# Three leading blocks' V by SyncE's queue in fp32 with a cast, and a new order of the first 340 tasks

## The chip, the core and the metric

The kernel runs on one core of one Trainium2 chip. A core has TensorE (PE) for matmuls, VectorE (DVE), ScalarE (ACT) and GpSimd (POOL) for the rest, SyncE (SP), which here only issues DMAs, and 16 DMA engines that all DMA queues share. PE writes its results to eight banks of PSUM, 128 x 512 fp32 each; DVE or ACT must empty a bank before it is used again. Every engine works through its own instructions strictly in order and waits at the first one whose inputs are not ready.

The metric is the time of one execution on the device in microseconds (us), lower is better.

## The reference

Eight heads of sliding-window attention with ALiBi, whose output goes as tokens into a feed-forward layer with squared ReLU:

```python
batch, n_heads, seq, head_dim = (8, 8, 576, 64)       # q, k, v in fp32
scores = scale * np.matmul(q, k.transpose(0, 1, 3, 2))
rel = pos[:, None] - pos[None, :]
bias = slopes[:, None, None] * (-np.abs(rel).astype(np.float32))[None, :, :]
mask = (rel >= 0) & (rel < 128)
scores = np.where(mask, scores + bias[None], -1000000000.0)
attn = np.exp(scores - np.max(scores, axis=-1, keepdims=True))
attn = attn / (np.sum(attn, axis=-1, keepdims=True) + 1e-09)
x = np.matmul(attn, v).transpose(0, 2, 1, 3).reshape(4608, 512)
h = x @ w_in                                          # 512 x 2048
out = np.maximum(h, 0.0) ** 2 @ w_out                 # 2048 x 512
```

## The kernel before

**Tiling.** Each sequence of 576 positions is cut into blocks of up to 128 positions by all 8 heads; the blocks are numbered in the order in which they are worked on. Blocks 0 to 3 are the first blocks of four sequences. They have no earlier block to look at and are called lone. Later blocks are "full" (they also look at the block before) or "half". The 4608 tokens are taken in nine groups g of 512 for the feed-forward layer. Group 0 (and with it blocks 0 to 3) is computed directly, in unit pieces; group 1 by unit pieces of twice the width; from group 2 on the first matrix product, and for all groups the second, is done by Strassen's seven products, with weight sums (us, ws) and token sums (ut, S1 to S4) made by DVE.

**Names of tasks.** Every piece of work is a task with a name; m is a block, g a group.

- `lk`, `lq`, `lv` load K, Q, V of a block. POOL's loads cast from fp32 to bf16 on the way. Block 0's K and Q go by SP's and ACT's queues in fp32 into a stage buffer (a part of the tile wsum), two halves each (`lk0.0`, `lk0.1`, `lq0.0`, `lq0.1`), and are cast by `ck0` and `cq0`.
- `tp m.0` and `tp m.1` transpose K and Q of a block on PE (four 128x128 matmuls each), `ev m.0.0` and `ev m.1.0` copy them out of PSUM.
- `b m` writes a lone block's ALiBi bias into two banks (two 128x512 matmuls); `s m` adds the scores, and for full blocks `s m.0` and `s m.1` are two bursts. `e m.i` is the exponential on ACT (lone: two; full: four), `m m.i` the multiplication by a mask on DVE for full blocks. The masks themselves (`mask part.head`) are 16 exponentials on ACT.
- `pv m.0`, `pv m.1` multiply by V, each for half of the heads; `r` and `n` are reciprocal and normalisation on DVE; `xp` transposes the result on PE and `x` copies it into xT.
- `u g.r.e` is a unit piece of x @ w_in: in group 0 r is one of four 128-token ranges, and e one of the pieces of w_in (2, 2, 4, 4, 4 chunks of 128 columns for r = 0; four of 4 chunks for the others). `relu...` is its ReLU on ACT, `squ...` its square.
- `w_in0` to `w_in4` load these pieces of w_in by POOL (two of 256 KB, three of 512 KB in bf16), `w_out0` to `w_out3` load w_out.
- `p g.i.z` is a Strassen product of the second matrix product.

**What sets the order.** The whole order is written out by hand in one string, ORDER, with a letter for the engine and the number of a PSUM bank or buffer (`s4.0::7,2`, `reluu0.1.0:a:0`). The planner takes the tasks in that order, checks that nothing comes before what it needs, and emits them; each engine's instruction stream is the part of ORDER with its letter. So a task that stands early in ORDER and waits for a load holds up everything behind it on its engine.

**Places that the steps touch.** PE starts with 12 warm-up matmuls (`warm`, line 662). Bias, scores and exponentials of lone blocks are lines 805, 814 and 823, transposes of K and Q 690, pv 874, xp 921, unit pieces 1021, their ReLU 988; copies go through a helper (428 on DVE, 430 on ACT). Block 0's stage loads are line 585, other K and Q loads of the first blocks 610, V loads 621, w_in 543, w_out 546. V of the blocks 0 to 3 has tiles of its own (vf), with a column of ones per head set by `one0.m`. K and Q of a block lie in a ring of four buffers (kq), so that the fifth block's load waits for the first block's transposes.

Of the kernel before, what the change touches and what calls it, by code (L numbers as in the profile page):

```python
# [25 lines left out]
N_XP = 13  # L26
N_CUT = 0
# [36 lines left out]
slope1.1:d slope0.1:a slope1.3:a ck0:a slope0.2:a warm::0 b0::1,2 lk2:g lq2:g lq0.0:s lq0.1:s lk1:g cq0:a one0.0:d  # L64
tp0.0::0 tp2.0::3 b2::4,5 tp0.1::6 tp2.1::7 ev2.0.0:d ev0.1.0:a lk3:g lq1:g tp3.0::3 ev3.0.0:a ev2.1.0:d ev0.0.0:d
one0.2:d tp1.0::6 s2 s0 e0.0:a e2.0:a e2.1:a ev1.0.0:d e0.1:a lv0:g lv2:g lq3:g lv1:g w_in1:g w_in0:g w_in2:g lv3:g
w_in3:g lk4:g lq4:g b1::0,3 tp1.1::6 pv2.0::4 ev1.1.0:d r2.0:d pv0.0::6 pv0.1::2 s1 n2.0:d r0.1:d r0.0:d n0.0:d
tp3.1::4 n0.1:d xp0.0::2 pv2.1::6 x0.0:d r2.1:d ev3.1.0:d mask1.1:a e1.0:a e1.1:a table:a pv1.0::0 pv1.1::3 b3::5,1
n2.1:d u0.0.1::2 r1.0:d r1.1:d n1.0:d n1.1:d xp2.0::6 s3 u0.0.0::0 xp1.0::3 dist0:d x2.0:a e3.0:a x1.0:a mask1.7:a
reluu0.0.0:a:0 u0.2.0::6 mask0.3:a mask1.2:a mask0.1:a mask1.6:a e3.1:a u0.1.0::3 u0.1.1::0 pv3.0::1 pv3.1::5  # L70
u0.2.1::4 u0.0.2::7 squ0.0.0:d one1.2:d reluu0.1.0:a:0 mask0.2:a reluu0.2.0:a:1 one1.8:d r3.0:d squ0.1.0:d one1.7:d
r3.1:d n3.0:d n3.1:d xp3.0::5 x3.0:d one1.5:d reluu0.2.1:a:0 one1.6:d squ0.2.1:d squ0.2.0:d reluu0.1.1:a:2 mask1.5:a
# [40 lines left out]
reluf2.2.4:a:0 sqf2.2.4:d sqc22.2.3:d c12.2.3:d:0 sqc12.2.3:d S2.2.0:d sqf2.1.4:a pv17.1::5 pv17.0::4 reluf2.3.4:a:3
sqf2.3.4:a st1.2.1:s st0.2.0:s st1.3.1:s st0.2.1:s st1.2.0:s st1.3.0:s kqT18:s x14:s x13:s x15:s x16:s kqT20:s kqT21:s
kqT22:s s18.0::1,2 s18.1::0,7 p2.2.0::3 p2.2.1 S1.2.1:d S2.2.1:d r17.0:d S4.2.1:d S3.2.1:d r17.1:d n17.0:d e18.0:a
e18.1:a s1_2:a:3 S3.2.0:d n17.1:d m18.0:d p2.5.0::2 p2.6.0 p2.5.1 p2.6.1 f3.0.1::5 f3.0.2::4 f3.1.1::1 s2_2:d:7
e18.2:a e18.3:a s1.3.0:a:5 ut3.0:d ut3.1:d m18.1:d ut3.2:d c11.3.0:d:0 ut3.3:d c11_2:d f3.0.5::7 f3.0.6 s2.3.0:a:1
# [198 lines left out]
def kernel(  # L316
    ctx: ExitStack, tc: tile.TileContext, q, k, v, moe_w_in, moe_w_out, out
):
    nc = tc.nc

    B, H, S, D = q.shape
    d_model = moe_w_in.shape[0]
# [88 lines left out]
    def tile_of(slot):  # L411
        return tiles[slot.tag][slot.idx]
# [110 lines left out]
    t_one = {}  # L523
# [39 lines left out]
    def load_block(m, key, v_key=None):  # L563
# [56 lines left out]
        def fetch_v():  # L620
            nc.gpsimd.dma_start(tile_of(s_v[m])[0:n, :, 0:D], source(v, m))  # L621
# [859 lines left out]
```

## Time and profile before

| | us |
|---|---|
| median of 3 runs (lowest to highest) | 287.59 (287.37 to 289.48) |
| the profiled execution | 288.0 |
| its span, first to last instruction | 285.9 |

| engine | busy us | share of the span |
|---|---|---|
| POOL | 106.3 | 37% |
| POOL's DMA queue | 18.10 MB | 87.8% of 16 engines' span |
| SP's DMA queue | 20.00 MB | 41.1% of 16 engines' span |

The busy time of a group of instructions counts pipelined matmuls in full, so a busy PE is not a PE at its peak: the time of a stretch of PE work is better read from the starts of what follows. The shares of the DMA queues add up the times of packets of which one engine has several under way, and so go over 100% in stretches. In POOL's timeline the time of a load is that of issuing it; when it has landed is told by the issues' median time to landing. A row such as `10.97 2.06 ACT ... x4 [0.65 <-PE s L814]` has start, length, engine, line, what is written from what, the count, and in brackets the idle time of the engine before it and what ended it.

### The profile page before, as it was taken

To read this page: it belongs to the slowest core of one execution; us is meant where nothing else is said; L and a number is where in the kernel's file an instruction comes from. 1 tells how busy PE (TensorE), PEld (TensorE's weight loads), DVE (VectorE), ACT (ScalarE), POOL (GpSimd) and SP (SyncE) were. 2 spreads that over 40 slices of the span, in tenths; PEclk is the share of its full clock that TensorE was granted. 3 is DMA by queue.
4 is the path that set the end of the run, shared out by engine and by line. 5 is a ranking of instruction groups with operands and counts; after the bars stand their busy time and mean duration, and the time that the engine had idled before them with its cause. 6 is when DMAs were issued, how large, how long until landed. Compare 5 with 4: busy or idle time off the path is not lost.

```text
span 285.9 us, 8500 instructions
## 1 busy us (share of the span) xinstructions
PE 277.0 (97%) x3403; PEld 240.0 (84%) x3404; DVE 247.1 (86%) x566; ACT 207.5 (73%) x408; POOL 106.3 (37%) x132
## 2 busy tenths in 40 slices
PE   6799999999999999999999999999999999999994
PEld 2588999888888888898888888889889888888883
DVE  2555898799999999999999899998999979998752
ACT  4579978986588993879779958686898655657300
POOL 8977645576567026580266253430000000000000
PEclk9999999999999999999999999999999999999998
DMA  9999999999999999999999999997531220031124
GB/s 126 161 197 167 183 201 165 171 172 148 206 145 250 131 172 129 149 207 130 203 135 150 139 174 164 170 164 157 148 93 39 40 73 3 0 111 39 53 79 127
DMA packets 169062, 39.08 MB, mean 137 GB/s; under 512 B 154560, under 2 KB 169024, under 8 KB 169024
## 3 DMA queue, kind: packets, MB, share of 16 engines
q0 software_dynamic: 115184, 18.10, 87.8%
q1 hardware_dynamic: 53248, 20.00, 41.1%
q8 instruction: 26, 0.43, 0.7%
q10 hardware_dynamic: 592, 0.46, 0.6%
q14 instruction: 12, 0.10, 0.1%
HBM read 36.70 MB, written 9.44 MB: 161 GB/s over the span
## 4 chain that ended last, share of the span: by engine, by line
PE 95%; ACT 2%; DVE 1%; issue 0%; POOL 0%; DVEq 0%; POOLq 0%
PE o L1271 38%; PE h L1116 30%; PE h L1021 9%; PE s L745 6%; PE pv L874 5%; PE wm L662 2%; PE xp L921 1%; PE tp L690 1%; ACT P L823 1%; ACT rt L988 1%; PE pv L856 1%; PE o L1373 0%; PE s L805 0%; ACT masks L475 0%; PE pv L851 0%; PE s L814 0%
## 5 line engine op out<-in xcount | busy, mean ns | idle before, releaser
L1271 PEld LDWEIGHTS <-g 128*128 128x128 bf16 x704 | 67.3, 98 | 9.0
L777 ACT ACTIVATE P<-s 128x512 bf16<-128x512 f32 x120 | 64.7, 613 | 5.7 <-PE s L745 3.3
L430 ACT ACTIVATE f<-h 128x512 f32<-128x512 f32 x74 | 42.5, 601 | 25.8 <-PE h L1116 25.5
L1137 DVE CUSTOM_DVE_ANT_0 rt<-h,f 128x512 bf16<-128x512 f32 x84 | 56.4, 684 | 4.9 <-ACT f L430 1.7
L980 ACT ACTIVATE g<-rt 128x512 bf16<-128x512 bf16 x79 | 48.4, 634 | 6.4 <-DVE rt L1137 5.9
L1271 PE MATMUL o<-w_out_sb,g 128*128 128x256 bf16 x432 | 52.3, 273 | 0.0
L1116 PE MATMUL h<-xT,w_in_sb 128*128 128x256 bf16 x336 | 46.9, 273 | 0.0
L1116 PEld LDWEIGHTS <-w_in_sb 128*128 128x128 bf16 x448 | 42.2, 98 | 5.6
L616 POOL DMA_DIRECT2D kq<-in_k_dram x24 | 21.5, 895 | 57.7 <-DMA kqT<-kq 54.7
L988 ACT ACTIVATE rt<-h 128x512 bf16<-128x512 f32 (+1 forms) x61 | 35.2, 599 | 8.6 <-PE h L1116 3.9
L1271 PE MATMUL o<-wsum,sums 128*128 128x256 bf16 x288 | 35.5, 273 | 0.0
L1116 PEld LDWEIGHTS <-us 128*128 128x128 bf16 x336 | 31.9, 98 | 4.3 <-DVE ut L1085 0.2
L1271 PE MATMUL o<-wsum,g 128*128 128x256 bf16 x272 | 34.5, 273 | 0.0
L772 DVE TENSOR_TENSOR P<-P,masks 128x1024 bf16<-128x1024 bf16 x48 | 32.2, 680 | 1.3 <-ACT masks L475 0.8
L1116 PE MATMUL h<-ut,us 128*128 128x256 bf16 x224 | 31.1, 273 | 0.0
L1021 PE MATMUL h<-xT,w_in_sb 128*128 128x128 bf16 (+1 forms) x384 | 30.8, 237 | 0.1
L982 DVE TENSOR_TENSOR g<-rt 128x512 bf16<-128x512 bf16 (+1 forms) x66 | 26.1, 413 | 4.7 <-ACT rt L988 4.4
L1271 PEld LDWEIGHTS <-sums 128*128 128x128 bf16 x288 | 27.5, 98 | 3.1
L901 DVE TENSOR_TENSOR x<-pv,rec 128x256 bf16<-128x256 f32 x72 | 28.7, 417 | 0.7
L1021 PEld LDWEIGHTS <-w_in_sb 128*128 128x128 bf16 x384 | 27.0, 98 | 2.3 <-issue 0.2
L621 POOL DMA_DIRECT2D vt<-in_v_dram x28 | 25.0, 908 | 7.8 <-PE pv L856 5.3
L430 ACT ACTIVATE f<-o 128x512 f32<-128x512 f32 x29 | 17.3, 599 | 11.0 <-PE o L1271 10.0
(84 smaller groups left out, 378.1 us busy)
## 6 DMA issues: line engine op xcount, KB each, us to landing
out_dram<-f SPq DMA_DIRECT2D x62, 128.0 KB, 3.9
kq<-in_k_dram POOLq DMA_DIRECT2D x31, 128.0 KB, 6.4
kq<-in_q_dram POOLq DMA_DIRECT2D x31, 128.0 KB, 7.2
vt<-in_v_dram POOLq DMA_DIRECT2D x28, 128.0 KB, 7.5
w_out_sb<-in_moe_w_out_dram POOLq DMA_DIRECT2D x4, 512.0 KB, 11.6
w_in_sb<-in_moe_w_in_dram POOLq DMA_DIRECT2D x3, 512.0 KB, 8.6
out_dram<-f SPq DMA_DIRECT2D x15, 64.0 KB, 2.1
vf<-in_v_dram POOLq DMA_DIRECT2D x4, 128.0 KB, 4.9
```

The costliest lines, as they stand in the source:

```text
L430: nc.scalar.activation(o, i, AF.Copy)
L621: nc.gpsimd.dma_start(tile_of(s_v[m])[0:n, :, 0:D], source(v, m))
L772: nc.vector.tensor_tensor(flat(Pt[sP.idx], w), flat(Pt[sP.idx], w), flat(mk, w), op=ALU.mult)
L777: nc.scalar.activation(flat(Pt[sP.idx], slice(2 * i, 2 * i + 2)), sS[i].tile.rearrange("p (j t) -> p j t", j=2)[:, :, lo:hi], AF.Exp, bias ...
L901: nc.vector.tensor_tensor(o, heads(sv)[0:n, :, 0:D], sr.tile[0:n, :].unsqueeze(2).to_broadcast([n, 4, D]), op=ALU.mult)
L980: nc.scalar.activation(o, i, AF.Square, bias=0.0, scale=1.0)
L982: nc.vector.tensor_tensor(o, i, i, op=ALU.mult)
L988: nc.scalar.activation(rts[srt.idx][:, 0:n], slot.tile[:, 0:n], AF.Relu, bias=0.0, scale=1.0)
L1021: nc.tensor.matmul(slot.tile[:, f * w:(f + 1) * w], w_in_sb[:, cc, fc * 128:(fc + 1) * 128], xT[:, cc, lo % (XR * 128):lo % (XR * 128) + w ...
L1116: nc.tensor.matmul(slot.tile[:, j * 256:j * 256 + 256], a, b_, start=fresh and j == 0 and c == 0, stop=c == 1, skip_group_check=True)
L1137: nc.vector._custom_dve(TENSOR_ADD_SAT, out=rts[srt.idx], in0=slot.tile, in1=other(), s0=FMAX, s1=0.0)
L1271: nc.tensor.matmul(slot.tile[:, z * 256:z * 256 + 256], stationary(c), moving(c), start=fresh and z == 0 and c == 0, stop=c == F - 1, skip ...
```

## The change

Two things change.

First, V of the blocks 0, 2 and 1 is no longer loaded and cast by POOL's queue. It is loaded by SP's queue in fp32 into stage buffers 1 to 3 (other parts of wsum), by one DMA per block in pieces of 256 bytes, and then cast to bf16 by a new task, `cv m`, on ACT (blocks 2 and 0) or DVE (block 1).

```diff
+V_HW = (0, 2, 1)
...
         def fetch_v():
             nc.gpsimd.dma_start(tile_of(s_v[m])[0:n, :, 0:D], source(v, m))
+        if m in V_HW:
+            st, s_sv = stages[1 + V_HW.index(m)][:, 0:d_model], Slot(f"stage{1 + V_HW.index(m)}")
+            l_v = plan.add({"SP": 720.0}, key + 0.2 if v_key is None else v_key,
+                           lambda: nc.sync.dma_start(st[0:n].rearrange("s (h d) -> s h d", h=H), source(v, m)), [],
+                           [s_sv], dma=700.0, lat=1500.0, name=f"lv{m}")
+            c_v = plan.add({"DVE": 590.0, "ACT": 480.0}, key + 0.2 if v_key is None else v_key,
+                           lambda: copy(c_v, tile_of(s_v[m])[0:n, :, 0:D], st[0:n].rearrange("s (h d) -> s h d", h=H)),
+                           [l_v], [s_v[m]], [s_sv], name=f"cv{m}")
+            t_load[m] = c_v
+            t_v[m] = [c_v, t_one["v0", m]]
+            return
```

Second, ORDER is rewritten up to the first products of group 0's second matrix product, about 340 tasks. Behind that the tasks and their order are the same; PSUM banks and a few buffers are renumbered throughout, consistently. POOL's loads now stand in this order:

```diff
-lk2 lq2 lk1 lk3 lq1 lv0 lv2 lq3 lv1 w_in1 w_in0 w_in2 lv3 w_in3 lk4 lq4 lk5 lk6 lq5 lv5 lq6 w_in4 lk7 lv4 lv6 lq7
-w_out3 w_out0 lv7 w_out2 w_out1 lkq8 lkq12 lkq9 lkq10
+lk2 lq2 lk1 lq1 lk3 lq3 w_in0 lv3 lk5 lq5 w_in1 lk4 lq4 w_in2 w_in3 lk7 lk6 lq6 w_in4 lv4 lv5 lq7
+w_out3 lv7 w_out2 lv6 w_out1 lkq8 lkq9 w_out0 lkq12 lkq10
```

PE's first tasks:

```diff
-warm b0 tp0.0 tp2.0 b2 tp0.1 tp2.1 tp3.0 tp1.0 s2 s0 b1 tp1.1 pv2.0 pv0.0 pv0.1 s1 tp3.1 xp0.0 pv2.1 pv1.0 pv1.1 b3
-u0.0.1 xp2.0 s3 u0.0.0 xp1.0 u0.2.0 u0.1.0 u0.1.1 pv3.0 pv3.1 u0.2.1 u0.0.2 xp3.0 u0.1.2 tp4.0 tp4.1 u0.2.2 s4.0 s4.1
+warm b0 tp0.0 tp0.1 b2 tp2.0 tp2.1 tp1.0 s0 tp1.1 s2 tp3.0 tp3.1 pv0.0 pv0.1 b1 s1 b3 pv2.1 xp0.0 pv1.0 s3 pv2.0 pv1.1
+tp5.0 pv3.0 xp2.0 pv3.1 u0.0.0 u0.0.1 tp5.1 tp4.0 xp1.0 u0.2.0 tp4.1 xp3.0 u0.1.0 s5.0 s4.1 s4.0 u0.3.0 s5.1 u0.2.1
```

ACT's, from the second cast of block 0's Q on:

```diff
-cq0 ev0.1.0 ev3.0.0 e0.0 e2.0 e2.1 e0.1 mask1.1 e1.0 e1.1 table x2.0 e3.0 x1.0 mask1.7 reluu0.0.0 ...
+cq0 cv2 ev0.1.0 cv0 ev0.0.0 e0.0 e0.1 e2.0 e2.1 ev3.1.0 e1.0 e1.1 mask1.1 mask1.0 e3.0 x0.0 e3.1 mask1.3 x2.0 ev5.0.0 ...
```

DVE's, up to block 0's normalisation:

```diff
-one0.0 ev2.0.0 ev2.1.0 ev0.0.0 one0.2 ev1.0.0 ev1.1.0 r2.0 n2.0 r0.1 r0.0 n0.0 n0.1
+one0.0 ev2.0.0 ev2.1.0 ev1.0.0 one0.2 cv1 ev3.0.0 ev1.1.0 r0.0 r0.1 n0.0 n0.1
```

Farther back in the rewritten part, the products p0.2, p0.1 and p1.1 of the second matrix product stand between the last unit pieces of group 1 instead of behind them, and some evacuations and squares change between ACT and DVE.

More of the change, by code (lines that the diff above doesn't have):

```diff
@@ L63 @@
 iota:g ident:d dist1:d slope1.0:d warm0:d lk0.1:a lk0.0:s one0.1:d slope0.3:d slope1.2:a slope0.0:a one0.3:d
[L64 to L72, printed above, removed]
@@ L113 @@
[L113 to L117, printed above, removed]
@@ L193 @@
-c11.8.2:d:0 c22.8.2:d:1 sqc11.8.2:a f8.2.4 sqc22.8.2:a c12.8.2:d:0 S1.8.0:d S3.8.0:d sqf8.0.4:d sqc12.8.2:d S1.8.1:d
-S2.8.0:d S3.8.1:d s5_7:a:1 reluf8.2.4:a:1 s2_7:a:6 p8.1.0::7 p8.1.1 p7.7.0 p7.7.1 sqf8.2.4:a c22_7:d s1_8:a:4
-sqf8.3.4:a p8.2.0::1 p8.2.1 c11_8:d S2.8.1:d p7.4.0 p7.4.1 p8.6.0 p8.6.1 p8.5.0::1 p8.5.1 st6.4.3:s st6.3.1:s
+slope1.1:d slope0.1:a slope1.3:a ck0:a slope0.2:a warm::0 b0::1,2 lk2:g lq2:g lq0.0:s lq0.1:s lv0:s lv2:s tp0.0::0
+cq0:a tp0.1::3 cv2:a b2::4,5 ev0.1.0:a one0.0:d lk1:g lq1:g lk3:g lq3:g lv1:s tp2.0::6 ev2.0.0:d tp2.1::7 cv0:a
@@ new lines @@
+ev2.1.0:d ev0.0.0:a tp1.0::3 s0 e0.0:a e0.1:a ev1.0.0:d one0.2:d cv1:d w_in0:g lv3:g lk5:g lq5:g w_in1:g lk4:g lq4:g
+tp1.1::3 s2 e2.0:a e2.1:a tp3.0::0 tp3.1::1 pv0.0::7 ev3.0.0:d pv0.1::2 ev3.1.0:a ev1.1.0:d b1::6,0 s1 e1.0:a e1.1:a
+b3::4,3 r0.0:d r0.1:d n0.0:d n0.1:d mask1.1:a pv2.1::5 xp0.0::2 pv1.0::6 r2.1:d r1.0:d s3 mask1.0:a e3.0:a pv2.0::1
+pv1.1::0 r2.0:d x0.0:a n2.0:d n2.1:d tp5.0::7 n1.0:d e3.1:a pv3.0::4 xp2.0::5 pv3.1::3 u0.0.0::6 u0.0.1::2 r1.1:d
+n1.1:d r3.0:d n3.0:d r3.1:d dist0:d tp5.1::0 mask1.3:a x2.0:a ev5.0.0:a tp4.0::7 xp1.0::4 u0.2.0::5 tp4.1::1 n3.1:d
@@ new lines @@
+x1.0:d xp3.0::3 u0.1.0::4 ev4.1.0:d ev5.1.0:d w_in2:g w_in3:g lk7:g lk6:g lq6:g w_in4:g lv4:g lv5:g lq7:g w_out3:g
+lv7:g w_out2:g lv6:g w_out1:g lkq8:g lkq9:g mask0.6:a reluu0.0.0:a:0 mask1.7:a ev4.0.0:a mask0.5:a mask0.2:a
+reluu0.2.0:a:1 mask1.6:a reluu0.0.1:a:2 reluu0.1.0:a:3 mask0.0:a x3.0:d squ0.2.0:d s5.0::0,1 e5.0:a s4.1::3,5
+s4.0::2,7 u0.3.0::6 e4.0:a mask1.5:a mask0.7:a e4.2:a mask0.1:a squ0.0.0:d s5.1::0,4 u0.2.1::2 u0.0.2::3 e5.1:a
+reluu0.2.1:a:0 reluu0.3.0:a:1 mask1.4:a mask1.2:a e4.1:a mask0.4:a one1.7:d u0.3.1::2 squ0.2.1:d e5.2:a mask0.3:a
@@ new lines @@
+s2.2.2:a:7 s17.1::0,1 f2.3.6 f2.1.4 f2.2.7 s5.2.2:a:2 e17.2:a f2.2.3 f2.3.5::0 sqc12.2.1:d sqc11.2.2:d S1.2.0:d
+s2.2.3:a:3 c22.2.2:d:3 sqc11.2.3:d reluf2.1.4:a:0 s5.2.3:a:2 f2.3.7 c12.2.2:d:1 c22.2.3:d:2 e17.3:a sqc22.2.2:a
+sqc12.2.2:d m17.1:d m17.0:d p2.1.0::7 f2.2.4 f2.3.4 p2.1.1 f2.3.3 s3_1:a:2 reluf2.2.4:a:1 sqf2.2.4:d sqc22.2.3:d
+c12.2.3:d:1 sqc12.2.3:d S2.2.0:d sqf2.1.4:a pv17.1::4 pv17.0::5 reluf2.3.4:a:3 sqf2.3.4:a st1.2.1:s st0.2.0:s
+st1.3.1:s st0.2.1:s st1.2.0:s st1.3.0:s kqT18:s x14:s x13:s x15:s x16:s kqT20:s kqT21:s kqT22:s s18.0::2,1 s18.1::6,3
@@ new lines @@
+m37.0:d s1.6.3:a:2 e38.0:a e38.1:a e38.3:a c11.6.3:d:1 sqc11.6.3:d m37.1:d m38.0:d s1.6.2:d:2 p5.4.0 f6.3.6 f6.2.2::6
+f6.3.5::2 pv37.0::4 pv37.1::1 c11.6.2:d:1 s2.6.3:a:3 f6.3.7 r37.1:d f6.2.6 p5.4.1 f6.2.5::6 e38.2:a s5.6.3:a:1
+c22.6.3:d:0 m38.1:d r37.0:d n37.0:d n37.1:d s2.6.2:a:2 sqc11.6.2:a f6.2.7 f6.3.3 st4.4.3:s x31:s x32:s st5.2.1:s
+st5.2.0:s st4.3.0:s x33:s st4.3.1:s st4.4.2:s x34:s s5.6.2:a:1 c22.6.2:d:1 f6.2.3 sqc22.6.3:a sqf6.0.4:a c12.6.2:d:0
+c12.6.3:d:2 f7.0.1::1 pv38::4,3 s3_5:a:1 sqc12.6.2:a f6.3.4 f7.1.1::7 pv36.0::2 r38.0:d n38.0:d r38.1:d n38.1:d
```

228 lines of the change are left out of this document (112 added, 116 removed).

## The prediction, made before the change was run

> **What bounds the kernel now.** I read the page first (span, shares, chain), then the stages, then PE's timeline of the first 33 us, then ACT's, then the landings of the first loads.
>
> ```profile
> span 285.9 us, 8500 instructions
> PE 277.0 (97%) x3403; PEld 240.0 (84%) x3404; DVE 247.1 (86%) x566; ACT 207.5 (73%) x408; POOL 106.3 (37%) x132
> PE 95%; ACT 2%; DVE 1%; issue 0%; POOL 0%; DVEq 0%; POOLq 0%
> 10.00:15.00 5.00, 3.39 (x61) 2.37 (x61) 2.91 (x11) 3.75 (x9) 5.00 (x8) 1.00 1.90 171
> 30.00:35.00 5.00, 5.00 (x116) 4.60 (x109) 4.04 (x15) 5.00 (x12) 3.24 (x5) 1.00 1.97 176
> ```
>
> TensorE is the bound, with 95% of the chain. The two rows of stages (length, then busy PE, PEld, DVE, ACT, POOL, then clock, DMA share, GB/s) say where it isn't full: 3.39 of 5 us in 10 to 15, all of it by 30. The reordered tasks hold the same matmuls, and the order behind them stays. So the change can move the end only by how much PE time it loses, mostly before about 32 us. To count that loss I need prices, from PE's timeline and (last five rows) the chain of waits:
>
> ```profile
> 2.50 5.17 PE L662 MATMUL wm<-sums 128*128 128x512 bf16 x12 [2.50 <-DVE sums L448]
> 7.50 0.60 PE L805 MATMUL s<-sums,ident 128*128 128x512 bf16 x2
> 7.93 0.61 PE L690 MATMUL tp<-ident,kq 128*128 128x128 bf16 x8
> 10.20 0.74 PE L814 MATMUL s<-kqf 64*128 64x128 bf16 x16
> ```
>
> ```profile
> 17.67 2.68 PE h L1021 x48
> 28.50 0.89 PE h L1021 x16
> 29.84 0.69 PE s L745 x16
> 32.09 1.89 PE h L1021 x32
> 37.64 0.48 PE pv L874 x16
> ```
>
> A bias pair b takes 0.43 (7.50 to 7.93), a transposing group tp or xp of four 0.225 (8.38 minus 7.93 is 0.45 for eight), a lone block's scores 0.37, a pv half 0.12 when eight matmuls become four, a unit piece u of four chunks 0.89 and of two 0.45, a full block's score burst 0.345. Warm-up ends at 7.50 in either order. At 17.67 PE had done 4 b, 8 tp, 4 lone s, 6 pv, 3 xp and 2 short u: 1.72+1.80+1.48+0.72+0.68+0.90 = 7.30 us. It had taken 10.17, so 2.87 were lost. At 32.09, with 4 b, 14 tp, 4 s, 8 pv, 4 xp, 2 short and 11 long u and 6 bursts (20.97 us), 3.62 were lost. Hence the ceiling of any gain: 3.6 us, and less than that by what ACT allows.
>
> **The change, part by part.** Three fp32 loads of V (blocks 0, 2, 1) go to SyncE's queue behind the q halves, and leave POOL's. Three casts are added: cv2 and cv0 on ACT, cv1 on DVE. On ACT the order becomes cq0, cv2, ev0.1.0, cv0, ev0.0.0, e0.0: SyncE's second load now stands ahead of the first block's evacuations.
>
> ```profile
> 2.10 0.60 SPq L585 DMA_DIRECT2D wsum<-in_q_dram  x1
> wsum<-in_q_dram SPq DMA_DIRECT2D x1, 128.0 KB, 4.2
> 1.34 1.02 POOL L610 DMA_DIRECT2D kq<-in_k_dram  x1 [0.16 <-issue]
> kq<-in_k_dram POOLq DMA_DIRECT2D x1, 128.0 KB, 5.1
> q0 software_dynamic: 854, 0.11, 84.6%
> q1 hardware_dynamic: 236, 0.22, 38.9%
> q0 software_dynamic: 4876, 0.62, 241.4%
> 5.82 0.92 POOL L621 DMA_DIRECT2D vf<-in_v_dram  x1
> vf<-in_v_dram POOLq DMA_DIRECT2D x1, 128.0 KB, 4.9
> 9.28 1.57 POOL L543 DMA_DIRECT2D w_in_sb<-in_moe_w_in_dram  x2
> w_in_sb<-in_moe_w_in_dram POOLq DMA_DIRECT2D x1, 256.0 KB, 5.7
> w_in_sb<-in_moe_w_in_dram POOLq DMA_DIRECT2D x1, 256.0 KB, 6.3
> 63.83 0.68 DVE L1341 TENSOR_TENSOR f<-o,f 128x512 f32<-128x512 f32 x1
> ```
>
> *The loads.* The second q half, issued at 2.10, landed at 6.3; POOL's first load, issued at 1.34, at 6.44, and its sixth, issued at 5.82, at 10.7: 0.86 apart, at POOL's issue rate. The third queue row (8 to 12 us) gives the engines' own rate: 4876 packets in 4 us, 1024 (one block's 128-byte pieces) in 0.84. In 3.25 to 5.25 (the two queue rows before it) the queues used 123.5% against 241.4% when full: half the engines' time, 0.97 us, was free. Three V loads are 3 x 1024 pieces of 256 bytes. At the same 0.84 each they need 2.52, 0.97 of it free, so POOL's loads behind them come 1.55 later than POOL's own rate would give: q3, the sixth, at 12.3. Then w_in0 (256 KB: two such pieces, issued at 9.28 and 10.02, landed at 15.0 and 16.3, so 1.34 each), v3, k5, q5 (0.84 each) and w_in1: 12.3+1.34+2.52+1.34 = 17.5. Without the free time it is 18.5, with V costing nothing 16.0.
>
> The Trainium skill ("DMA: Bandwidth & Descriptors", Issuing engines are not separate DMA queues) says that DMAs of all issuing engines run on the same 16 engines and interleave, so that spreading them saves issue time only. By it the V loads cost their full 2.52, w_in1 lands at 18.5, 0.1 after PE's arrival below, and the sum would be 288.6. It speaks against the change; the row of stores beside POOL's loads, below, agrees with it.
>
> *When V lands.* No row shows a SyncE load of 1024 pieces. From below: issued behind q0.1 at about 2.7 (lv0) and 3.4 (lv2) with q's 4.2, lv2 lands at 7.6. From above, the two nearest kinds on that queue:
>
> ```profile
> q1 hardware_dynamic: 582, 0.54, 104.7%
> q0 software_dynamic: 17, 0.00, 2.0%
> out_dram<-f SPq DMA_DIRECT2D x1, 128.0 KB, 4.9
> out_dram<-f SPq DMA_DIRECT2D x3, 128.0 KB, 1.8
> L676 SPq DMA_TRANSPOSE kqT<-kq x7: 1232/1934/3269, 47.4 to 69.2; - x7
> DMA to landing us min/median/max: 5.2/6.8/8.5
> ```
>
> A store of 128 KB lands in 1.8 us when POOL's queue is empty (200 to 205 us) but in 4.9 beside it (83 us); in 88 to 89.5 us SyncE's packets ran nearly alone (582 to 17) while POOL's stood. So the engines serve roughly by order of issue, and a load waits for what was issued before it. A transpose of kq takes 1.2 us at least to issue and 5.2 to 8.5 to land: lv2 issued at 4.0 would land at 9.2 to 12.5. I take 9.3: q0.1's 6.33, three loads of 0.84 (lv0, lv2 and one of POOL's between), and half of another. The bounds for lv2 are 7.6 and 12.5.
>
> *ACT and PE from there.*
>
> ```profile
> 6.41 0.63 ACT L430 ACTIVATE kq<-wsum 128x512 bf16<-128x512 f32 x1 [1.50 <-DMA wsum<-in_q_dram]
> 9.23 1.09 ACT L430 ACTIVATE kqf<-tp 128x512 bf16<-128x512 bf16 x2 [2.20 <-PE tp L690]
> 10.97 2.06 ACT L823 ACTIVATE P<-s 128x512 bf16<-128x512 f32 x4 [0.65 <-PE s L814]
> 22.50 1.30 ACT L475 ACTIVATE masks<-sums 128x128 bf16<-128x128 f32 x6
> 39.63 1.13 ACT L777 ACTIVATE P<-s 128x512 bf16<-128x512 f32 x2
> 54.74 1.04 ACT L430 ACTIVATE kqf<-masks 128x1024 bf16<-128x1024 bf16 x1
> ```
>
> A 128x512 pass paces at 0.515 (2.06/4), a mask at 0.2. The first fp32 cast took 0.63, about as long. cv2 starts at 9.35; with ev0.1.0, cv0 and ev0.0.0 behind it (4 x 0.5) ACT is through at 11.35, where the old order ended its two evacuations at 10.3. s0 runs at 11.55, e0.0 starts at 12.1. Seven passes (four e, ev3.1.0, e1.0, e1.1) and two masks take it to 16.1. e3.0 needs s3, which PE's order puts behind pv1.0, and so behind e1.0 (15.2): s3 is out by then. With e3.0, x0.0 and e3.1 it is 17.7. Then pv3.1, u0.0.0 (0.45), and u0.0.1 starts at 18.4; w_in1 (17.5) is there. By then PE has done 4 b, 9 tp, 4 s, 8 pv, 2 xp and one short u: 7.09 us in 10.9, 3.81 lost against 2.87 at 17.67 before. That is +0.94.
>
> *What costs nothing.* cv1 (0.68, by DVE's fp32 sum above) waits for lv1 with ev3.0.0 and ev1.1.0 queued behind it on DVE; k3 lands only at about 11.4, so about 1 us of cover; beyond that every us goes to s1. POOL loses three issues of 0.9, but its landings follow the engines. SyncE has nothing behind lv1 until its first transpose at 47. The stage buffers lie in wsum, whose next writers, the weight sums, come after the units. Later loads, with a 512 KB piece as twice 1.34: w_in2 21.9, w_in3 24.5, w_in4 29.7, v4 30.6, each ahead of its user: before u0.3.3, the first to need w_in4, PE has 19.4 us of work, so it is there at 7.5+19.4+3.8 = 30.7, and at pv4.0 two long u later. Between 18 and 32 I let the loss grow as before (0.75).
>
> **The sum.** The profiled execution took 288.0 (span 285.9 and 2.1 around it), 0.4 above the median 287.59. 288.0 + 0.94 = 288.94, less 0.4: 288.5.
>
> **Rivals.**
> *B, V in time.* If lv2 is there at 8.5, ev0.1.0 starts when tp0.1 is out (8.38 and 0.2), ev0.0.0 is through 1.25 earlier, u0.0.1 starts at 17.15 if w_in1 is there, and 2.56 are lost: 0.3 better than before. With no growth between 18 and 32 it is 1.05 better. 286.5 to 287.3, say 286.9. For it: engines half free until 5.25. Against: three loads' 2.5 us, and w_in1 at 17.5. More isn't in it: from 8.58 ACT has 7 us of passes before pv3.1, so even this order can't save 2.9 us.
>
> *C, V late, ACT blocked.* The price is one for one: each us of lv2 after 9.3 moves ev0.1.0, s0, all exps and u0.0.1. Beyond 11.3 it costs over 1% (0.94+2.0). By the transposes' median lv2 lands at 10.8 (+2.4), by their worst at 12.5 (+4.1). PE would then stand nearly idle from 9.1 to over 12, and the warm-up shows what a cold array costs: 12 matmuls of 512 in 5.0 us, 0.42 each, against 0.215 for the same shape right after 7.50. One such slow stretch adds about 1 us. 290.5 to 292.5, say 291.5. For it: the trace's transposes, and packets of one queue standing while the other's run. Against: q0.1's 4.2 at the very moment.
>
> On that clock the Trainium skill ("TensorE: Matmul & The Clock Gate", Part 1) says that an idle window of about 3.4 us halves it; by that the slow stretch would be at least that long. The trace has no such window behind the warm-up to show it: PE's 3.39 of 5 us in 10 to 15 went at clock 1.00.
>
> *D, ACT's queue later.* From e3.1 to e7.3 ACT's new list has 37 passes, 14 masks, two half passes (0.3) and pm0 (1.04, which stood later): 19.1+2.8+0.6+1.04 = 23.5 us from 17.1, ending at 40.6, against 40.76 before, without any idle time. ACT was full there already (5.00 of 5). If it slips by one block's four exps (2.06) with 8 banks taken, PE stands 2 to 3 us: 291. For it: the order is new and PE is strictly in order. Against: PE reaches e7's scores only at about 37.
>
> *E, nothing moves*: V's loads and casts fit as the old ones did, 287.6.
>
> **Numbers.** Forecast 0.40 (lv2 between 8.5 and 11.3), B 0.13, C 0.30, D 0.12, E 0.05. About 1% (2.9 us) is what a measurement of this kernel can tell from no change. C and D are slower by that: 0.42. Of B's 0.13 I give 0.02 to a gain over 1%, which its account doesn't allow. The rest, 0.56, is within. The range takes in B's middle and most of C and D: 286.5 to 292.0, leaving out about 0.06 below and 0.12 above.
>
> **What will show it.** The start of ACT's third cast from wsum is lv2's landing: 9.3 right, under 8.6 B, over 11.3 C. PE's first h matmuls: 18.0 for u0.0.0. POOL's w_in landings: 13.6 and 17.5. A row of PE waiting for ACT between 20 and 45 us of over 1 us is D; clock under 1.00 in 10 to 20 us is C's second part. I am wrong in the ledger if the end moves by other than the loss counted at 32 us.

## The result, and the profile after

The changed kernel takes 291.80 us (median of 4 runs, 291.41 to 293.39) against 287.59 for the kernel before beside it: a ratio of 1.0137, 95% interval 1.0097 to 1.0177. That is the prediction's rival C in time (291.5), not its forecast (288.5). The profiled execution took 293.39 us with a span of 290.8; the one before had 285.9. It was the longest of the four: the other three had spans of 289.6 to 290.0, so what is read below from the profile is about 1 us more than an ordinary run lost.

The stages (the columns are those of the two rows of stages in the prediction; the last three are granted clock, DMA share and GB/s), two of the kernel before and then those of the changed kernel:

```profile
10.00:12.50 2.50, 1.93 (x33) 1.26 (x32) 1.31 (x5) 1.85 (x5) 2.50 (x5) 1.00 2.35 154
17.50:20.00 2.50, 2.50 (x49) 2.50 (x46) 0.38 (x3) 2.48 (x10) 0.94 (x2) 1.00 1.63 192
```

```profile
7.50:10.00 2.50, 2.34 (x21) 1.38 (x19) 0.35 (x2) 0.01 (x1) 1.62 (x3) 1.00 1.75 189
10.00:12.50 2.50, 0.31 (x4) 0.30 (x4) 0.41 (x2) 1.48 (x3) 1.79 (x3) 1.00 2.09 156
12.50:15.00 2.50, 1.35 (x26) 0.90 (x24) 0.47 (x2) 2.01 (x5) 0.88 (x1) 1.00 1.55 174
15.00:17.50 2.50, 1.79 (x18) 1.01 (x16) 2.03 (x7) 1.29 (x3) 1.93 (x3) 0.52 2.28 160
17.50:20.00 2.50, 2.50 (x27) 1.66 (x28) 0.28 (x3) 1.48 (x4) 2.12 (x3) 0.50 1.93 176
20.00:22.50 2.50, 2.30 (x35) 1.81 (x33) 1.74 (x7) 1.93 (x5) 2.19 (x4) 0.62 1.71 191
22.50:25.00 2.50, 2.50 (x48) 2.50 (x46) 1.96 (x8) 2.09 (x7) 1.32 (x2) 1.00 1.25 207
```

PE works 0.31 of 2.5 us in 10 to 12.5 (1.93 before), and from 15 to 22 us it is granted half its clock. A row of "2.50, 2.50 (x27)" at clock 0.50 looks full, but holds 27 matmuls where the same stage of the kernel before held 49: busy time doesn't show the loss, the count and the clock do. From 22.5 on the clock is full again. Three lines of PE's timeline, and one of the chain of waits, place the loss:

```profile
9.23 0.61 PE L703 MATMUL tp<-ident,kq 128*128 128x128 bf16 x8
12.19 0.38 PE L703 MATMUL tp<-ident,kq 128*128 128x128 bf16 x4 [2.35 <-ACT kqf L432]
22.34 1.05 PE L1034 MATMUL h<-xT,w_in_sb 128*128 128x128 bf16 x16
```

```profile
35.52 1.89 PE h L1034 x32
```

By the prediction's ledger PE had done, before the unit pieces that start at 22.34, 4 b, 9 tp, 4 s, 8 pv and 2 xp (1.72+2.03+1.48+0.96+0.45 = 6.64 us): 22.34-7.50-6.64 = 8.2 us lost. Before the piece u0.3.3 at 35.52 it had done 15 tp, 4 xp, 2 short and 9 long u and 6 bursts beside those (19.42 us): 8.6 lost. The kernel before had lost 3.62 at 32.09. The difference of 4.98 is the span's 4.9: 8.2 of the 8.6 are lost ahead of 22.3 us, and behind 35.5 nothing is.

What PE, ACT and DVE waited for (the first three lines from PE's waits: us in total, times, longest; then ACT's and DVE's timelines):

```profile
PE tp L703 <- ACT kqf L432: 2.4, 1, 2.4
PE tp L703 <- DMA kq<-in_k_dram: 0.5, 1, 0.5
PE tp L703 <- DMA kq<-in_q_dram: 0.5, 1, 0.5
```

```profile
6.88 0.63 ACT L432 ACTIVATE kq<-wsum 128x512 bf16<-128x512 f32 x1 [1.97 <-DMA wsum<-in_q_dram]
11.03 0.63 ACT L432 ACTIVATE vf<-wsum 128x512 bf16<-128x512 f32 x1 [3.52 <-DMA wsum<-in_v_dram]
11.56 0.58 ACT L432 ACTIVATE kqf<-tp 128x512 bf16<-128x512 bf16 x1
13.63 2.06 ACT L836 ACTIVATE P<-s 128x512 bf16<-128x512 f32 x4 [0.49 <-PE s L827]
15.12 0.43 DVE L430 CAST vf<-wsum 128x512 bf16<-128x512 f32 x1 [2.04 <-DMA wsum<-in_v_dram]
```

The third cast from wsum (ACT's second line) starts at 11.03: lv2 is there 1.7 us later than the 9.3 taken. ACT had stood 3.52 us for it, with the first block's evacuation behind it, and PE behind that. DVE stood 2.04 us for lv1. And the loads, issue and landing (the first and the third of SyncE's V loads, then POOL's sixth, q3, by its timeline and its issue's row, the us to landing last; then q3 in the chain of waits):

```profile
2.75 0.59 SPq L627 DMA_DIRECT2D wsum<-in_v_dram  x1
wsum<-in_v_dram SPq DMA_DIRECT2D x1, 256.0 KB, 6.5
4.14 3.25 SPq L627 DMA_DIRECT2D wsum<-in_v_dram  x1
wsum<-in_v_dram SPq DMA_DIRECT2D x1, 256.0 KB, 11.0
5.83 0.92 POOL L612 DMA_DIRECT2D kq<-in_q_dram  x1
kq<-in_q_dram POOLq DMA_DIRECT2D x1, 128.0 KB, 9.8
```

```profile
5.83 9.78 DMA kq<-in_q_dram
```

lv0 lands at 9.25 and lv1 at 15.1; issuing lv1 alone held SyncE for 3.25 us. POOL's sixth load lands 9.8 us after its issue, at 15.6, where before it took 4.9 (10.7) and 12.3 was predicted. So V came late, and all that POOL loads came late with it. Which of the two cost the time, what of it is the clock, and what the new order itself does, the trace alone can't say: PE waits for one thing at a time, and behind each wait stands the next.

### The profile page after: what moved, and what is told of

Read it like the earlier page. It is cut to its first block, busy times and chain, and to the rows that moved or that the text cites. A ratio compares the mean times of both kernels' runs of the same rounds, so it can differ in the third digit from the quotient of the medians.

```text
span 290.8 us, 8518 instructions
## 1 busy us (share of the span) xinstructions
PE 279.6 (96%) x3403; PEld 241.7 (83%) x3404; DVE 246.1 (85%) x564; ACT 210.7 (72%) x413; POOL 103.7 (36%) x129
## 4 chain that ended last, share of the span: by engine, by line
PE 90%; DMA 3%; ACT 2%; POOL 2%; DVE 1%; issue 0%; DVEq 0%; POOLq 0%
PE o L1284 38%; PE h L1129 30%; PE h L1034 8%; PE s L758 6%; PE pv L887 5%; DMA kq<-in_q_dram 3%; POOL kq L612 2%; PE xp L934 1%; ACT P L790 1%; ACT rt L1001 1%; PE s L818 1%; PE tp L703 1%; PE pv L869 1%; ACT masks L477 0%; PE o L1386 0%; PE s L827 0%
## 5 line engine op out<-in xcount | busy, mean ns | idle before, releaser
L1001 ACT ACTIVATE rt<-h 128x512 bf16<-128x512 f32 (+1 forms) x61 | 35.5, 601 | 10.2 <-PE h L1129 3.9
L995 DVE TENSOR_TENSOR g<-rt 128x512 bf16<-128x512 bf16 x66 | 26.2, 415 | 5.7 <-ACT rt L1001 5.3
## 6 DMA issues: line engine op xcount, KB each, us to landing
w_out_sb<-in_moe_w_out_dram POOLq DMA_DIRECT2D x4, 512.0 KB, 11.4
```

Source lines behind the costliest of these rows:

```text
L995: nc.vector.tensor_tensor(o, i, i, op=ALU.mult)
L1001: nc.scalar.activation(rts[srt.idx][:, 0:n], slot.tile[:, 0:n], AF.Relu, bias=0.0, scale=1.0)
```

## The experiments

Theory 1: SyncE's three V loads take much more from POOL's loads than 1.55 us, and PE follows the K and Q that come late. Theory 2: the new order itself costs. Theory 3: ACT stands at a cast of V with the evacuations behind it. Theory 4: a part is the halved clock. All times below are medians, the ratios are against the kernel before run beside each (its medians were 287.59 for the change and 287.94 to 288.11 for the others).

| run | median us | ratio | 95% interval |
|---|---|---|---|
| the change | 291.80 | 1.0137 | 1.0097 to 1.0177 |
| order alone, V by POOL | 290.28 | 1.0080 | 1.0052 to 1.0109 |
| V by SyncE alone, old order | 292.63 | 1.0157 | 1.0122 to 1.0193 |
| the change, V not loaded | 286.76 | 0.9943 | 0.9918 to 0.9968 |
| the change, casts on DVE | 292.58 | 1.0147 | 1.0105 to 1.0188 |
| the change, PE kept busy | 290.78 | 1.0099 | 1.0070 to 1.0129 |
| before, one extra load | 289.41 | 1.0041 | 1.0022 to 1.0060 |
| before, two | 290.23 | 1.0085 | 1.0042 to 1.0128 |
| before, three | 292.57 | 1.0148 | 1.0111 to 1.0185 |
| before, three in long rows | 290.72 | 1.0082 | 1.0048 to 1.0116 |
| before, one at the start | 289.84 | 1.0075 | 1.0058 to 1.0093 |
| the change, third V by POOL | 290.26 | 1.0069 | 1.0046 to 1.0092 |
| order, V by POOL, tp later | 290.05 | 1.0083 | 1.0060 to 1.0105 |

### The halves of the change

The order alone, V on POOL's queue without casts:

```diff
-V_HW = (0, 2, 1)
+V_HW = ()
-... lk2 lq2 lk1 lq1 lk3 lq3 w_in0 ...        (POOL)
+... lk2 lq2 lk1 lq1 lv0 lk3 lq3 lv2 lv1 w_in0 ...
```

> The new order with V's three loads back on POOL's queue in bf16 and no casts. Theory 1 (SyncE's V loads hold up POOL's loads and PE with them): POOL's loads land about 0.86 us apart again, the seventh (q3) at about 11.6 us, the first w_in piece near 15; the warm clock holds and the time is 286.5 to 288.5 us. Rival 2 (the order of the 340 tasks itself costs): 290 to 292 us, with PE's loss arising between 20 and 45 us or from the order of its first bursts.

V by SyncE alone, in the old order:

```diff
+V_HW = (0, 2, 1)
-... lq1:g lv0:g lv2:g lq3:g lv1:g w_in1:g ...
+... lq0.1:s lv0:s lv2:s lv1:s ... lq1:g lq3:g w_in1:g ...
+... ev1.0.0:d cv2:d cv0:d ... ev3.1.0:d cv1:d
```

> The old order with the three V loads on SyncE's queue; their casts stand on DVE, late, so no evacuation on ACT waits for V. Theory 1 (loads displaced): q3 lands at about 15 us, against 10.7 before, scores of block 3 and the first piece of w_in follow it, and the time is 290 to 292 us. Rival 3 (ACT's queue standing behind the cast of V is the cause): the transposes' evacuations run by 10.3 us as before, and the time is 287.3 to 288.5 us.

V by SyncE alone costs as much as the whole change (1.0157; 292.63 us, above the 290 to 292 that theory 1 expected), though no evacuation waits there for V to land: theory 1, and against theory 3. PE waits 2.3 us for a load of K in it, and 1.2 us for a cast of V that stands late in DVE's order. Yet the order alone isn't free: 1.0080 and 290.28 us, in the band of the rival and not in theory 1's 286.5 to 288.5. POOL's loads land about 0.86 apart in it, as theory 1 said, and the first wait is no longer the casts'; but PE then waits elsewhere, and the clock isn't kept (half from 18.0 to 21.4 us). Its waits in the run of the order alone:

```profile
PE tp L702 <- DMA kq<-in_k_dram: 2.0, 1, 2.0
PE pv L886 <- DMA vf<-in_v_dram: 0.6, 1, 0.6
PE h L1033 <- DMA w_in_sb<-in_moe_w_in_dram: 0.4, 1, 0.4
```

The new order asks for block 5's K at 15.3 us, ahead of the unit pieces, and it comes at 17.2: with three V loads more in POOL's queue it is the twelfth there, not the ninth. That miss put the question of what the order is worth when V costs nothing. The next kernel leaves the three loads out and multiplies by other values in place of V; only its time is of use:

```diff
-            st, s_sv = stages[1 + V_HW.index(m)][:, 0:d_model], Slot(f"stage{1 + V_HW.index(m)}")
-            l_v = plan.add({"SP": 720.0}, ...)
+            st = stages[0][:, 0:d_model]
...
-                           [l_v], [s_v[m]], [s_sv], name=f"cv{m}")
+                           [t_kq[0][0], t_kq[0][1]], [s_v[m]], [], name=f"cv{m}")
```

> The changed kernel without the three loads of V on SyncE's queue: V of blocks 0, 2 and 1 is not loaded, and the three casts read the first K half's fp32 instead (the casts and the new order stay). Theory 1 (the loads of V are the whole cost): POOL's sixth load (q3) lands at about 10.7 us, w_in1 at about 16, the clock stays warm, and the time is 286 to 287.8 us. Rival (the new order or the casts cost of themselves): 289 us or more.

0.9943: with the three loads gone, and casts and order kept, the kernel takes 0.6% less than the one before, about 1.6 us; rival B had allowed 1.05 on its best account. That is no gain at equal work, since the kernel before loads these blocks too, on POOL's queue. What it shows is that the loss doesn't lie in the casts or the order by themselves, and that the three loads, with all that follows from them (the halved clock too: here it is 1.00 throughout), cost the change from 0.9943 to 1.0137, some 5.6 us. The order is built on V for nothing, and loses as soon as V is paid for, by either queue. (In details the expectation missed: q3 landed at 11.9, not 10.7, w_in1 at 17.1.)

### ACT's queue or the loads

The two casts on ACT were put on DVE, so that ACT's evacuations run as soon as the transposes are out:

```diff
-... cq0:a cv2:a ev0.1.0:a cv0:a ev0.0.0:a ...
+... cq0:a ev0.1.0:a ev0.0.0:a ...   one0.2:d cv0:d cv2:d cv1:d ...
```

> The changed kernel with the casts of block 2's and block 0's V moved from ACT to DVE, so that ACT's evacuations no longer stand behind a load of V. Theory 1 (loads displaced): block 0's scores come up to 2 us earlier, but PE then stands behind k1, k3 and q3 in its own order; 290 to 291.8 us. Rival 3 (ACT's queue): block 0's exps start at about 10.5 us and the time falls to 287.5 to 289 us.

1.0147: no gain (292.58 us, above both bands). PE's waits in that run:

```profile
PE tp L703 <- DMA kq<-in_k_dram: 3.5, 2, 1.9
PE tp L703 <- DMA kq<-in_q_dram: 0.9, 2, 0.7
```

The 2.4 us of waiting for ACT have become 3.5 and 0.9 us of waiting for K and Q (k1 lands at 11.2, q1 at 12.65, k3 at 15.0). Where a wait's cause is moved away and the time stays, that wait was one of several and not the one that sets the time. Theory 3 falls.

### The clock

In the changed kernel the clock is halved from 15.1 to 21.9 us (0.52 and 0.62 in the first and the last of its three rows of 2.5 us, 0.50 between). Extra matmuls fill PE's waits; nothing reads what they write:

```diff
+WARM_TP = {(2, 1): 22, (3, 0): 5, (1, 1): 4}
...
+                whole = st.tile
...
+                for _ in range(WARM_TP.get((m, i), 0)):
+                    nc.tensor.matmul(whole[:, 256:512], warm[:, 0:128], warm[:, 0:256], start=True, stop=True)
```

> The changed kernel with 31 extra matmuls of 256 columns on PE behind the transposes of blocks 2, 3 and 1, into half a bank that nothing reads; they fill idle time while PE waits. Theory 4 (a part of the loss is the halved clock of 15 to 22 us): the granted clock stays at 1.00 behind 8 us and the time is 289.3 to 290.5 us. Rival (the waits for loads cover the slow stretch, so that the clock costs nothing): 291.5 to 292.5 us at the same clock of 1.00.

The stages of that run from 15 us, and its first unit piece:

```profile
15.00:17.50 2.50, 2.45 (x36) 1.64 (x35) 1.64 (x6) 2.08 (x5) 2.18 (x3) 1.00 2.33 159
17.50:20.00 2.50, 2.05 (x40) 1.44 (x37) 1.80 (x8) 2.50 (x9) 1.95 (x3) 1.00 1.93 177
```

```profile
20.09 0.61 PE L1038 MATMUL h<-xT,w_in_sb 128*128 128x128 bf16 x8
```

At a clock of 1.00 (36 matmuls in 15 to 17.5, a few of them extra, instead of 18) the first unit piece starts at 20.09, 2.25 us before the changed kernel's 22.34, and the profiled span is 2.0 us shorter (288.8). Over the timed runs the gain is less, 1.0099 against 1.0137, about 1.1 us, with intervals that overlap; 290.78 is just above the expected band. The changed kernel's other three runs had spans of 289.6 to 290.0, so a part of the 2.0 belongs to the one that was profiled. This puts the clock at one to two us of the loss; by the timed runs alone it isn't clear of noise.

The halved stretch is not the changed kernel's alone, and this bears on the runs that follow. In their profiles the clock is 0.50 for 3.4 us with the order alone, V by SyncE alone, two and three extra loads, one load at the start and the third V by POOL, and for 6.8 us in the changed kernel and with the casts on DVE; it stays at 1.00 from the end of the warm-up on with one extra load, three in long rows, no V, and the transposes later. What 3.4 us of it go with can be seen in the kernel before: of its 20 runs beside the extra loads four were granted a mean clock of 0.994, as one such stretch in 286 us gives, and took 289.35 to 289.51 us; the other 16 took 287.26 to 288.73. So a step of about 1.5 us between two of these rows can be the clock, whatever else a load does.

### What a load on the second queue costs

Extra loads on SyncE's queue in the kernel before, of the changed kernel's kind and place, that nothing early reads; V still comes by POOL, and order and casts are the old ones:

```diff
+        extra = [plan.add({"SP": 720.0}, 0.0, lambda j=j: nc.sync.dma_start(
+                     stages[1 + j][:, 0:d_model].rearrange("s (h d) -> s h d", h=H), source(v, (0, 2, 1)[j])),
+                     [], [], dma=700.0, lat=1500.0, name=f"lx{j}") for j in range(3)]
-... lq0.1:s ...
+... lq0.1:s lx0:s lx1:s lx2:s ...
```

> The kernel before with three extra loads on SyncE's queue behind the q halves, the same 3 x 1024 pieces of 256 bytes into the same stage buffers; nothing early reads them, and V still comes by POOL. So only their load on the engines is added: no cast, no wait for V, no new order. Theory 1: POOL's sixth load lands 4 to 5 us later than 10.7, and the time is 290 to 292 us. Rival (a wait for V is what costs): POOL's loads 1.5 us later at most, 287.5 to 288.5 us.

> As the run with three extra loads, but one. If each load costs POOL's stream the same: its sixth load 1.4 to 1.6 us later than 10.7, time 288.5 to 289.5 us. If the free half of the engines before 5.25 us takes the first one: under 0.7 us later, 287.5 to 288.2 us. If the cost arises only as long as both queues run beside each other, it is more for one than a third of three: over 1.7 us later.

> As the run with three extra loads on SyncE's queue, but two. One put POOL's sixth load 1.2 us later, three 4.6. If each load behind the first costs 1.7: 2.9 us later, 290 to 291 us. If it is the third, which is issued in pieces while its queue is full, that costs most: 2.4 us or less, under 290 us.

| extra loads | POOL's first load lands | its sixth | later than before's sixth | ratio of times |
|---|---|---|---|---|
| none | 6.44 | 10.72 | | 1 |
| one | 6.63 | 11.91 | 1.2 | 1.0041 |
| two | 5.99 | 13.01 | 2.3 | 1.0085 |
| three | 6.68 | 15.29 | 4.6 | 1.0148 |
| three in long rows | 6.45 | 14.41 | 3.7 | 1.0082 |

Three loads that nobody waits for cost what the change costs, with no cast, no wait for V and no new order (292.57 us, above the 290 to 292 of theory 1). The first two put POOL's sixth load 1.2 and 1.1 us later, the third 2.3; as its first load scatters by 0.7 us, single steps are good to some tenths only. One extra load lay between its expectations: less than the 1.4 to 1.6 of an equal share, more than the 0.7 of a free half. Two extra loads gave 2.3 later, as the guess that the third costs most had it, but at 290.23 us, just over its 290.

Why so much, the packets of the two queues show (packets, MB, share of 16 engines; q0 is POOL's, q1 SyncE's). First 12 to 13 us of the run with one extra load, when only POOL's queue is still at work on short pieces; then the same microsecond of the run with three; last the changed kernel:

```profile
q0 software_dynamic: 1227, 0.15, 243.0%
```

```profile
q0 software_dynamic: 414, 0.05, 79.5%
q1 hardware_dynamic: 412, 0.11, 79.4%
```

```profile
q0 software_dynamic: 405, 0.06, 80.4%
q1 hardware_dynamic: 403, 0.10, 77.6%
```

In this microsecond the two queues' packets go through one to one, together 826 instead of 1227, and POOL's stream runs at a third of its pace. The bytes don't fall: 0.05 and 0.11 MB are as much as the 0.15 of POOL alone, as SyncE's packets leave twice as many bytes each. Nor is one to one the rule. From 7 to 8 us the run with three loads had 575 packets of SyncE's and 520 of POOL's (0.14 and 0.07 MB), and the changed kernel:

```profile
q1 hardware_dynamic: 970, 0.25, 116.1%
q0 software_dynamic: 103, 0.01, 18.9%
```

So what POOL loses is best counted in bytes. The prediction's row of 8 to 12 us has 0.62 MB in 4 us; at that rate 256 KB take 1.7 us and three such loads 5.1, an estimate, against 4.6 measured.

The engines' share falls from 243% to 159% while both queues have loads outstanding. A low share is no sign of room here. That was the reading that failed: the prediction took 123.5% in 3.25 to 5.25 us, with POOL's and SyncE's loads both under way, for half-free engines. In bytes its own rows show no such room: 0.11 and 0.22 MB in those 2 us, 0.165 a microsecond, against 0.155 in 8 to 12. The Trainium skill ("DMA: Bandwidth & Descriptors", Queues, rings and completion order) says that an engine goes round robin over its queues packet by packet; 414 and 412 agree with it, 970 and 103 by themselves don't; whether the page's packet is one of the trace's isn't shown.

Bytes or pieces? The same 768 KB in rows of 2 KB:

```diff
-    stages[1 + j][:, 0:d_model].rearrange("s (h d) -> s h d", h=H), source(v, (0, 2, 1)[j])
+    stages[1 + j][:, 0:d_model], v.rearrange("b h s d -> (b h s d)")[j * 65536:(j + 1) * 65536].rearrange("(s e) -> s e", e=512)
```

> As the run with three extra loads, but the same 3 x 256 KB in rows of 2 KB (128 rows a load). If bytes are what the engines are short of: POOL's sixth load is as late as with the short pieces, and the time is within 0.5 us of that run. If the count of packets is: POOL's sixth load moves by under 1.5 us, and the time is 287.5 to 288.3 us.

An eighth of the pieces, and POOL's sixth load is still 3.7 us later (4.6 with short ones): neither expectation holds, but bytes carry most of it. An fp32 block of V is 256 KB, as much as w_in0, for which the prediction had a price of 1.34; three are 4.0. The other 0.9 is little more than the scatter of 0.7, so that the piece count costs anything isn't shown by it. The time falls by more (1.0082 against 1.0148, about 1.9 us), and there the clock has its part: with the short pieces it is half from 17.4 to 20.8 us, with the long rows it stays at 1.00.

One load in the free half that the prediction saw, issued by ScalarE at 1.5 us:

```diff
+... lk0.1:a lx0:a ...
```

> The kernel before with one extra load of 1024 pieces of 256 bytes on ScalarE's queue as its second transfer, issued at about 1.4 us, into a stage buffer that nothing early reads. If half of the engines' time before 5.25 us is free (the prediction's 0.97 us): POOL's sixth load lands at most 0.4 us later than 10.7 and the q halves hardly later; 287.4 to 288.2 us. If the long rows of k and q already take all that the engines can move (190 to 205 GB/s): the second q half lands about 1.2 us later than 6.3 and POOL's sixth load 1 us or more; 288.7 to 290 us.

The second q half landed at 7.39 (6.33 before), POOL's sixth load at 11.48 (0.8 later), and the time rose by 0.75%: between the two for POOL's load, on the side of no free time for the q half and for the total. But the total is no measure of the load here. PE's start on block 0 hangs on that half, and came 0.5 us later (8.44 against 7.93); PE's waits are those of the kernel before, and at 15 us it is still 0.5 behind. Then comes half clock, from 15.3 to 18.7 us, and behind it the long run of unit pieces starts at 19.42 instead of 17.51:

```profile
15.00:17.50 2.50, 2.45 (x25) 1.91 (x26) 1.99 (x9) 0.45 (x2) 2.14 (x3) 0.56 1.32 205
17.50:20.00 2.50, 2.50 (x39) 2.11 (x37) 0.82 (x3) 1.57 (x3) 0.94 (x2) 0.76 1.65 190
```

So of 1.9 us behind, 1.4 came with the clock.

### Two ways to save it

The third load, the dearest, back to POOL in the changed kernel:

```diff
-V_HW = (0, 2, 1)
+V_HW = (0, 2)
-... lk3 lq3 w_in0 ...      one0.2:d cv1:d
+... lk3 lq3 lv1 w_in0 ...  one0.2:d
```

> The changed kernel with the third load of V (block 1) back on POOL's queue behind q3, without its cast; the first two stay on SyncE's queue. If the third load costs twice as much as each of the first two, because it goes out in pieces beside POOL's packets (three extra loads put POOL's sixth load 4.6 us later, two 2.3): q3 lands at 13 to 13.5 us, SyncE's issues take under 0.9 us each, and the time is 290 to 291 us. If the loads cost alike (1.6 each): q3 at 13.9 to 14.4 us, 291 to 291.8 us. If the waits of ACT for the first two loads are what binds, no change: 291.5 to 292 us.

q3 at 13.3, 290.26 us, SyncE's issues at 0.72 or less, as the first expectation had it: half of the loss is gone with one of three loads, 3.4 us of half clock among it. On SyncE's queue the third load puts POOL's stream back by 15.6-13.3 = 2.3 us; on POOL's own queue it takes 0.9 (v1 lands at 14.2).

And the order with V by POOL, with the transposes of blocks 5 and 4 and their loads behind the first unit pieces:

```diff
-... pv1.1 tp5.0 pv3.0 xp2.0 pv3.1 u0.0.0 u0.0.1 tp5.1 tp4.0 xp1.0 u0.2.0 tp4.1 xp3.0 u0.1.0 s5.0 ...
+... pv1.1 u0.0.0 u0.0.1 pv3.0 xp2.0 pv3.1 xp1.0 u0.2.0 xp3.0 u0.1.0 tp5.0 tp5.1 tp4.0 tp4.1 s5.0 ...
-... w_in0 lv3 lk5 lq5 w_in1 lk4 lq4 ...
+... w_in0 w_in1 lv3 lk5 lq5 lk4 lq4 ...
```

> The new order with V on POOL's queue again, and the four transposing groups of blocks 5 and 4 moved behind the first five unit pieces of blocks 0, 2 and 1, their loads behind w_in1 and v3, so that PE has units to do while k5 is on its way. If PE's 2.2 us of waiting for k5 in the run of the order alone was a matter of the sequence: 286.5 to 288.3 us, and no wait for a K load over 0.5 us. If the bytes are simply not there by then, the wait moves to another load (w_in0, w_in1 or w_in2) and the time stays at 289 to 290.5 us.

Its waits of PE:

```profile
PE h L1033 <- ACT P L835: 1.4, 1, 1.4
PE tp L702 <- ACT kqT L431: 0.9, 1, 0.9
PE s L757 <- DVE kqT L429: 0.5, 1, 0.5
```

No wait for a load is left, and the clock stays at 1.00, but 290.05 us: PE now waits for the exponentials ahead of the first units and for the evacuations behind the bundled transposes. Neither expectation's reason holds: the wait moved, but to ACT and DVE, not to another load. No version here that loads V beat the kernel before.

## Why the prediction came out as it did

- **The range held, the likeliest case did not.** 291.80 lies in 286.5 to 292.0, and "slower by over 1%" had 0.42; but 0.56 stood on "no change", and the forecast of 288.5 is 3.3 us short. That the range held is due to its being drawn wide enough to take in most of rival C.
- **The step that failed** is the pricing of the three loads, the 1.55 us by which POOL's loads were to come later. The mechanism (V's loads displace POOL's) was right, the size wrong: 4.6 us for three loads measured alone, and in the change q3 at 15.6 instead of 12.3, w_in0 at 16.9 instead of 13.6, w_in1 at 20.8 instead of 17.5. The 0.84 a load is the price of 1024 pieces that leave 128 bytes each; these bring 256. Nor were the 0.97 free. Not all of the lateness is theirs: without any V q3 came at 11.9 in this order, not at 10.7, so the three loads are 3.7 of the 4.9 there.
- **lv2's landing** of 9.3 was 11.0, inside its bounds (7.6 to 12.5). 0.5 of that was there at q0.1 (6.8 instead of 6.33); the rest fits the same price, but was not taken apart.
- **Rival C** foretold the time, by V late (11.0, at its price 1.7 us, is 290.2) and a cold array (1 us, measured 1 to 2). Its limit of 11.3 was not reached, and its reason is half right: with ACT freed of the casts the time stayed. K and Q were as late as V, which C left out, so that its number came so close is in part luck.
- **The Trainium skill's rule** on issuing engines ("DMA: Bandwidth & Descriptors", Issuing engines are not separate DMA queues) had given 288.6 by the full 2.52: right that a second queue is no second set of engines, and still short, as 2.52 was worked out at 0.84 a load.
- **The clock gate.** The Trainium skill ("TensorE: Matmul & The Clock Gate", Part 1) has the halved clock come after an idle window of about 3.4 us and the slow stretch last at least that long; the trace has PE idle but for four matmuls from 9.8 to 13.2 and half clock for 6.8 us from 15.1 on, so the length agrees. The idle window is not borne out in all runs: with one load at the start the clock fell at 15.3 though PE was busy for 1.97 of the 3.4 us before, and with the long rows it stayed full at 11.9 behind 1.62 of 3.4. What makes it fall stays open.
- **The ledger** was right to a tenth: the loss counted ahead of u0.3.3 grew by 4.98, the span by 4.9.
- **Rivals B, D, E.** B's account of the order agrees with the run without V loads (0.9943), but B wanted V loaded and in time, and no run had that. D did not happen: ACT is full from 25 to 35 us, but the longest wait of PE for it there is 0.2. E neither: something moved.
- **"cv1 costs nothing"**: it took k3 to be at 11.4; k3 came at 14.7 and lv1 at 15.1, so DVE's 2.04 us at cv1 were covered to 0.4.

## What to carry to other kernels

Before a load is moved to a second queue, price it in bytes at its new type, at the nearest row of that size, and count nothing as free because the engines' share is low while two queues have loads outstanding: look at the bytes that a microsecond moves, alone and together. When two versions differ by a us or so, compare the granted clock by stages before the difference is put down to the change. When PE stands at one late thing, ask which thing is late next, and test it by taking the first away. An order that is written for a resource that comes free of charge is worth only what that resource really costs.

## What the hardware showed that was not expected

- Two queues at work on short pieces at once moved 826 packets in the microsecond shown, one alone 1227, but as many bytes: 0.16 and 0.15 MB.
- The clock was halved for 3.4 us in a run whose PE had been busy for 1.97 of the 3.4 us before, and not in one with 1.62; 1.4 us were lost with it.
- SyncE's third load took 3.25 us to issue, against 0.59 for the first of the same shape; in the run with three extra loads the third took 3.25 too, and 0.43 in long rows, an eighth of the pieces. So it goes with the number of pieces; whether with its own or those queued ahead of it was not tried.
- Three loads of the same bytes in an eighth of the pieces put POOL's stream back by 3.7 instead of 4.6 us, a difference near the scatter: most of the cost goes with the bytes.
